# Eight gate products are issued before 32 up products instead of behind them

## The chip, the cores and the metric

The kernel runs on one core of a Trainium2 chip. The metric is the device time of one execution in microseconds (us). The engines of the core are TensorE (PE, with its weight loads as PEld), VectorE (DVE), ScalarE (ACT), GpSimd (POOL) and SyncE (SP), which issues the transfers. Each of ACT, DVE and POOL carries out its instructions in the order in which the program lists them.

## The reference

Three layers follow each other on 2 sequences of 768 tokens: a recurrent attention (mLSTM, 8 heads of 40), a gated MLP with a spatial mix (gMLP), and a channel mix. What matters here is the second layer, and that the third uses it:

```python
h = np.maximum(x @ w_in, 0.0)                       # x: (2, 768, 320), w_in: 320 x 1024
u, v = h[..., :512], h[..., 512:]
mu, var = np.mean(v, -1, keepdims=True), np.mean((v - mu) ** 2, -1, keepdims=True)
v_n = (v - mu) / np.sqrt(var + 1e-06)
v_s = np.einsum('ts,bsd->btd', w_spatial, v_n) + b_spatial[None, :, None]
x = (u * v_s) @ w_out                               # w_out: 512 x 320
# channel mix: token shift, k = relu(xk @ w_k)**2, out = sigmoid(xr @ w_r) * (k @ w_v)
```

## The kernel before

The kernel computes in float32 by pairs: each operand of a product is split into a high half (rounded to the form that TensorE takes) and a low half (what is left), and a product is a sum of high*high, high*low and low*high. So each input of a product needs two writes: a cast by ACT (high) and a subtraction by POOL or DVE (low).

The tokens come in 12 chunks of 128. Chunks 0 to 5 are sequence 0, chunks 6 to 11 are sequence 1; the attention takes them in the order 0, 6, 1, 7, ... 5, 11. When a chunk's attention output is transposed (`turn`), two kinds of product become possible:

- **vp** (`vpart`, one per chunk, 8 matmuls of 512 columns): x @ w_in's second half. Behind it runs a chain: ACT relu from PSUM into `vr` (L718), DVE statistics (L705, L720), POOL root (L710, L711), DVE normalise (L724), ACT cast to the high half of `vn` (L726), POOL subtraction for its low half (L234, out `vn`). `vr` has two buffers.
- **up** (`upart`, four per pair of chunks, 8 matmuls of 256 columns each): the first half of w_in, with one ACT relu into `u` (L739).

They lie in a list, `fillers`, one entry per matmul, and are issued one or a few at a time between the attention's steps. An entry holds the function, its planned cost (0.229 us for a vp matmul, 0.107 for an up matmul), and the keys it must wait for. When the attention has issued its last step, what is left in the list is issued at once. At that point these are: the rest of vp4, vp10, vp5, the four up products of the pair (4, 5), called up2, then vp11, then the four of the pair (10, 11), called up5.

Before they go out, the kernel queues the splitting of w_out (`widen("w_o", ...)`, four pieces; name `wo`). A piece comes as raw bits by a transfer into one of two `wraw` buffers; ACT and DVE turn it to float32 (L273, L274, L278, L282), ACT casts it to the high half (L290), POOL subtracts (L234, out `wo`). The tiles `wo` take pages of a ring of 12, and the first write to them (the cast of piece 0) waits for the last reader of the page it takes over: that is a matmul of vp11, which reads the high half of w_in's second half (`w_v`) there.

Behind the last up comes the spatial mix, four runs `s0` to `s3` of four products `spp`, 18 matmuls each: `s0` and `s1` (both halves of w_spatial) read the six `vn` chunks of sequence 0, `s2` and `s3` those of sequence 1. In a product the low half of chunk 5 is read last, by matmul 18, and its high half first by matmul 16. The whole order is `s0 K1 s1 r o0 K0 s2 v x o1 s3 o2`: `o` is the w_out product (`wop`), `K`, `r` and `v` queue the splitting of w_k, w_r and w_v. The second half of w_spatial (`wsp`, six pieces, also through `wraw`) is split during `s0`. Then come the channel mix's products `kp`, `rp` and, last, `vv` with w_v.

The order of work of the four compute engines is written out by a planner inside the kernel: it keeps a clock for each engine from estimated costs (the first number of every step), and issues the step of the chain that can start first. The order on ACT, DVE and POOL thus follows from the order in which TensorE's products are put out.

The products take eight PSUM banks in turn, six from one pool and two from another; a bank is free when the ACT or DVE step that reads it is done.

Of the kernel before, what the change touches and what calls it, by code (L numbers as in the profile page):

```python
# [17 lines left out]
def tile_mlstm_gmlp_channelmix(  # L18
# [64 lines left out]
    class Chain:  # L83
# [14 lines left out]
        def eta(self, k):  # L98
            t = self.ready
            for s in self.steps:  # L100
                t = max(t, free.get(s[0], 0.0)) + s[1] + HOP
                if len(s) > 3 and s[3] == k:
                    break
            return t
# [70 lines left out]
    def finish(*keys, stall=True):  # L175
        for k in keys:
            while any(b[0] == k or b[0][0] == k for b in back):
                if not force_feed():
                    break
            for c in [c for c in running if c.has(k)]:  # L180
                while c in running and c.has(k):
                    advance(c.start(), skip=c)
                    if not c.open():
                        finish(split[0], stall=False)
                    if c in running and c.has(k):
                        issue(c)
        if stall:
            at_least(max([done.get(k, 0.0) for k in keys], default=0.0))
# [246 lines left out]
    def arrival(i):  # L435
        return max(st["at", i], st["rows", i, 0] - 0.9) if i is not None else 0.0
# [343 lines left out]
    fillers = []  # L780

    later = []

    def fill(n, lag=1e9):
        for _ in range(n):
            if fillers and eta(fillers[0][2]) > clock[0] + lag:
                break
            if not fillers and later:
                fillers.extend(later)
                later.clear()  # L790
            if fillers:
                fillers.pop(0)[0]()
# [194 lines left out]
    while todo:  # L987
# [9 lines left out]
        if best is None:  # L997
            if fillers and eta(fillers[0][2]) <= clock[0] + 0.1:
# [3 lines left out]
                        key=lambda t: max(eta(t["keys"]), arrival(t["arrive"])))  # L1002
# [21 lines left out]
    for j in range(4):  # L1024
        widen("w_o", wo[0][:, j, :DM], ((wo[1][:, j, :2 * P], slice(0, 2 * P)), (wo[0][:, j, DM:], slice(2 * P, DM))), w_out[j])
    closing.append(0)
    fill(len(fillers) + len(later))
    finish(*[c.key for c in running if not c.late], stall=False)

    at.release()  # L1030
# [298 lines left out]
```

## Time and profile before

| what | value |
|---|---|
| median of 3 runs | 313.67 us (313.42 to 313.88) |
| profiled execution, own time | 313.5 us |
| its span, first to last instruction | 311.8 us |
| PE busy | 298.6 us, 96% of the span |
| PEld busy | 283.4 us, 91% |
| DVE / ACT / POOL busy | 71% / 53% / 49% |
| mean granted TensorE clock | 0.982 |
| chain that ended last, share of PE | 80% |

The span is what the trace covers; the execution's own time has 1.7 us more. The chain that ended last is followed back from the last instruction to whatever released each step; where it names an engine other than PE, that engine held TensorE up.

### The profile page before, as it was taken

The numbers are of one execution on the slowest core, as the hardware profiler recorded it, in microseconds if no ns is written. First come the engines' busy times: TensorE is split into PE (matmuls) and PEld (weight loads), VectorE is DVE, ScalarE is ACT, GpSimd is POOL, SyncE is SP. The second block draws the span as 40 slices with busy tenths as digits, with TensorE's granted clock in tenths as the row PEclk, the third lists the DMA queues.
The fourth block names the chain that finished last, engine by engine and source line by source line (L and its number), as shares of the span: only waits on it lengthen the run. The fifth ranks groups of instructions, "written<-read, shape, count | busy, mean of one in ns | idle before, by whom it ended". The sixth has DMA issues, their size and how long they took to land.

```text
span 311.8 us, 5519 instructions
## 1 busy us (share of the span) xinstructions
PE 298.6 (96%) x2010; PEld 283.4 (91%) x2010; DVE 220.8 (71%) x432; ACT 165.6 (53%) x348; POOL 153.5 (49%) x197
## 2 busy tenths in 40 slices
PE   8899987799999999979999999999999999999995
PEld 6777876698988998979999999999999999999994
DVE  7799895764658668466798999898867755745611
ACT  3645778534746533453444474586955744734610
POOL 5174557933768944582483736563625404403500
PEclk9999999599999999979999999999999999999999
DMA  5959663343341301135222511231010010001001
GB/s 153 300 163 312 224 230 98 114 115 110 91 144 52 125 30 39 47 126 178 104 84 62 182 44 52 79 125 42 3 41 26 0 42 23 0 23 42 0 23 43
DMA packets 13938, 28.75 MB, mean 92 GB/s; under 512 B 2407, under 2 KB 7783, under 8 KB 13911
## 3 DMA queue, kind: packets, MB, share of 16 engines
q1 hardware_dynamic: 13879, 28.33, 29.3%
q8 instruction: 16, 0.26, 0.4%
q0 software_dynamic: 32, 0.07, 0.1%
q14 instruction: 11, 0.09, 0.1%
HBM read 26.20 MB, written 1.97 MB: 90 GB/s over the span
## 4 chain that ended last, share of the span: by engine, by line
PE 80%; DVE 6%; ACT 4%; POOL 4%; issue 2%; DMA 1%; SPq 1%; DVEq 0%; ACTq 0%; POOLq 0%
PE spp L649 16%; PE kp L649 14%; PE vv L649 14%; PE wop L649 7%; PE up L649 6%; PE vp L649 5%; PE rp L649 5%; PE av L576 4%; PE sc L456 2%; PE ip L556 2%; PE sp L522 2%; PE ld L487 1%; DMA og<-in_o_tok_dram 1%; POOL vn L234 1%; PE tp L624 1%
## 5 line engine op out<-in xcount | busy, mean ns | idle before, releaser
L649 PE MATMUL spp<-wsp,vn 128*128 128x384 f32 x288 | 52.6, 342 | 1.6 <-ACT vn L726 0.8
L649 PEld LDWEIGHTS spp<-wsp,vn 128*128 128x128 f32 x288 | 51.4, 193 | 2.2 <-ACT vn L726 1.2
L1172 POOL TENSOR_TENSOR sq<-sq 128x384 f32<-128x384 f32 x32 | 29.9, 940 | 47.2 <-ACT sq L1171 47.2
L649 PE MATMUL kp<-xk,wk 128*128 128x384 f32 x256 | 45.3, 334 | 0.0
L649 PEld LDWEIGHTS kp<-xk,wk 128*128 128x128 f32 x256 | 44.4, 188 | 0.0
L649 PE MATMUL vv<-wv,k 128*128 128x320 f32 x288 | 42.9, 309 | 0.0
L649 PEld LDWEIGHTS vv<-wv,k 128*128 128x128 f32 x288 | 42.4, 188 | 0.0
L234 DVE TENSOR_TENSOR k<-sq,k 128x384 fp32r<-128x384 f32 x32 | 26.2, 820 | 13.6 <-ACT k L1173 13.6
L1069 POOL TENSOR_TENSOR vs<-vs,u 128x384 f32<-128x384 f32 x16 | 19.8, 1244 | 19.7 <-DVE vs L1068 19.7
L649 PE MATMUL up<-xg,w_u 128*128 128x256 f32 x192 | 29.2, 291 | 0.0
L649 PE MATMUL vp<-w_v,xg 128*128 128x512 f32 x96 | 28.4, 410 | 0.1
L278 DVE SCALAR_TENSOR_TENSOR wbits<-wsq,wbits 128x320 int32<-128x320 int32 (+1 forms) x27 | 22.3, 829 | 6.0 <-ACT wsq L273 5.2
L649 PEld LDWEIGHTS up<-xg,w_u 128*128 128x128 f32 x192 | 25.4, 190 | 0.5
L576 PE MATMUL av<-kvq,dt 128*128 128x123 f32 (+1 forms) x192 | 25.6, 279 | 0.1
L576 PEld LDWEIGHTS av<-kvq,dt 128*128 128x128 f32 x192 | 24.7, 197 | 1.0 <-issue 0.3
L1171 ACT ACTIVATE sq<-kp 128x384 f32<-128x384 f32 x32 | 15.6, 490 | 16.2 <-PE kp L649 14.1
L649 PE MATMUL wop<-gt,wo 128*128 128x384 f32 x128 | 22.8, 334 | 0.0
L649 PEld LDWEIGHTS wop<-gt,wo 128*128 128x128 f32 x128 | 22.2, 188 | 0.0
L649 PEld LDWEIGHTS vp<-w_v,xg 128*128 128x128 f32 x96 | 17.1, 189 | 3.0 <-DVE xg L234 0.5
L1212 DVE TENSOR_TENSOR ob<-rs,vv 128x320 f32<-128x320 f32 x12 | 5.8, 487 | 19.7 <-PE vv L649 18.7
L234 POOL TENSOR_TENSOR vn<-vr,vn 128x512 fp32r<-128x512 f32 x12 | 15.8, 1313 | 5.4 <-ACT vn L726 5.3
L282 DVE SCALAR_TENSOR_TENSOR wsq<-wraw,wbits 128x320 int32<-128x320 int32 (+1 forms) x21 | 18.2, 870 | 0.3
(182 smaller groups left out, 565.9 us busy)
## 6 DMA issues: line engine op xcount, KB each, us to landing
kvq<-in_kvq_dram SPq DMA_DIRECT2D x10, 516.0 KB
qk<-in_qk_dram SPq DMA_DIRECT2D x24, 160.0 KB
wraw<-in_w_k_dram SPq DMA_DIRECT2D x6, 512.0 KB
wraw<-in_w_v_dram SPq DMA_DIRECT2D x8, 320.0 KB
wraw<-in_w_sp_dram SPq DMA_DIRECT2D x12, 192.0 KB
og<-in_o_tok_dram SPq DMA_DIRECT2D x12, 160.0 KB
out_dram<-ob SPq DMA_DIRECT2D x12, 160.0 KB
w_inv<-in_w_in_dram SPq DMA_DIRECT2D x3, 512.0 KB
```

The source lines that it names most:

```text
L234: eng.tensor_tensor(out=out, in0=a, in1=b.bitcast(F32), op=ALU.subtract)
L278: vec.scalar_tensor_tensor(out=t["bits"], in0=t["sq"].bitcast(I32), scalar=3, in1=t["bits"], op0=ALU.logical_shift_left, op1=ALU.bitwise_or)
L282: vec.scalar_tensor_tensor(out=t["sq"].bitcast(I32), in0=t["high"], scalar=SIGN, in1=t["bits"], op0=ALU.bitwise_and, op1=ALU.bitwise_or)
L456: pe.matmul(st["sc", i, x][:, h * P:(h + 1) * P], k_[64 * x:64 * x + D, h, :], q_[64 * x:64 * x + D, h, :], start=True, stop=True)
L522: pe.matmul(sp[:n * D, h0 * DA:(h0 + n) * DA], kw[:, h0:h0 + n, :].rearrange("p h d -> p (h d)"), vt[:, h0:h0 + n, :].rearrange("p h d -> ...
L556: pe.matmul(ip[:, h0 * DA:(h0 + n) * DA], qt[:n * D, g, :], cs[:n * D, h0 * DA:(h0 + n) * DA], start=True, stop=True)
L576: pe.matmul(av[:, own_, :], A[:, h, :], vt[:, own_, :], start=True, stop=True)
L649: pe.matmul(out[0], l, x, start=j == 0, stop=j == len(prs) - 1)
L1069: ("P", 1.29, lambda: pool.tensor_tensor(out=vs, in0=vs, in1=ut[b][:, d, sl], op=ALU.mult)),
L1171: chain(("k2", g, f), ("A", 0.49, lambda: act.activation(out=sq, in_=ps, func=AF.Relu), ("kp", g, f)), ("P", 0.96, lambda: pool.tensor_ten ...
L1172: ("P", 0.96, lambda: pool.tensor_tensor(out=sq, in0=sq, in1=sq, op=ALU.mult)),
L1212: vec.tensor_tensor(out=ob, in0=rs, in1=ps, op=ALU.mult)
```

## The change

Where the rest of the list is issued, it is now sorted first: from the first entry that begins a product or waits for something, all entries with a planned cost of 0.2 or more (the vp matmuls) go ahead of those below (the up matmuls). The sort keeps the order within each kind.

```diff
     closing.append(0)
-    fill(len(fillers) + len(later))
+    rest = fillers + later
+    begun = next((x for x, f in enumerate(rest) if f[2]), 0)
+    fillers.clear()
+    later.clear()
+    fillers.extend(rest[:begun] + sorted(rest[begun:], key=lambda f: f[1] < 0.2))
+    fill(len(fillers))
     finish(*[c.key for c in running if not c.late], stall=False)
```

On TensorE, behind vp5, this is the first product before (up2_0; the number behind a name is a tile's own):

```order
L649 MATMUL vp5_1622<-w_v1_149,xg2_1338 128x512
L649 MATMUL up2_0_1652<-xg2_1338,w_u0_623 128x256
L649 MATMUL up2_0_1652<-xg2_1338,w_u1_624 128x256
L649 MATMUL up2_0_1652<-xg2_1338,w_u0_623 128x256 x2
L649 MATMUL up2_0_1652<-xg2_1338,w_u1_624 128x256
```

And at the same place after:

```order
L649 MATMUL vp5_1622<-w_v1_149,xg2_1338 128x512
L649 MATMUL vp11_1652<-w_v0_148,xg5_1457 128x512
L649 MATMUL vp11_1652<-w_v1_149,xg5_1457 128x512
L649 MATMUL vp11_1652<-w_v0_148,xg5_1457 128x512 x2
L649 MATMUL vp11_1652<-w_v1_149,xg5_1457 128x512
L649 MATMUL vp11_1652<-w_v0_148,xg5_1457 128x512 x2
L649 MATMUL vp11_1652<-w_v1_149,xg5_1457 128x512
L649 MATMUL up2_0_1678<-xg2_1338,w_u0_623 128x256
```

Only vp11 has moved: ahead of the 32 matmuls of up2. Behind up5 the products are the same as before.

On ACT, from the relu of vp5 (`vr5`) to the cast of chunk 5's high half (`vn1_0<-vr5`), before:

```order
L718 ACTIVATE vr5_1650<-vp5_1622 128x512
L739 ACTIVATE u0_942<-up2_0_1652 128x256
L739 ACTIVATE u0_942<-up2_1_1661 128x256
L726 CAST vn3_0_1497<-vr10_1618 128x512
L273 ACTIVATE wsq_1693<-wraw_1642 128x320
L739 ACTIVATE u0_942<-up2_2_1676 128x256
L290 CAST wo0_1590<-wsq_1629 128x320
L739 ACTIVATE u0_942<-up2_3_1690 128x256
L290 CAST wo0_1590<-wsq_1693 128x320
L273 ACTIVATE wsq_1727<-wraw_1668 128x320
L718 ACTIVATE vr11_1722<-vp11_1708 128x512
L726 CAST vn1_0_1348<-vr5_1650 128x512
```

And after:

```order
L718 ACTIVATE vr5_1650<-vp5_1622 128x512
L290 CAST wo0_1590<-wsq_1629 128x320
L726 CAST vn3_0_1497<-vr10_1618 128x512
L273 ACTIVATE wsq_1672<-wraw_1642 128x320
L718 ACTIVATE vr11_1676<-vp11_1652 128x512
L739 ACTIVATE u0_942<-up2_0_1678 128x256
L739 ACTIVATE u0_942<-up2_1_1687 128x256
L739 ACTIVATE u0_942<-up2_2_1699 128x256
L290 CAST wo0_1590<-wsq_1672 128x320
L739 ACTIVATE u0_942<-up2_3_1714 128x256
L726 CAST vn1_0_1348<-vr5_1650 128x512
```

The relu of vp11 (`vr11`) stood directly ahead of that cast and behind two preparations of w_out pieces (`wsq_1693`, `wsq_1727`); it now stands ahead of the four relus of up2, and the preparation of the last piece has gone behind the cast.

On POOL, from the low half of chunk 10 (`vn3_1<-vr10`) to the low half of chunk 5 (`vn1_1<-vr5`), before:

```order
L234 TENSOR_TENSOR vn3_1_1498<-vr10_1618,vn3_0_1497 128x512
L710 TENSOR_TENSOR sb5_1651<-sb5_1651,eps_71 128x1
L711 TENSOR_TENSOR sb5_1651<-sb5_1651,eps_71 128x1
L234 TENSOR_TENSOR wo1_1591<-wsq_1629,wo0_1590 128x256
L234 TENSOR_TENSOR wo0_1590<-wsq_1629,wo0_1590 128x64
L234 TENSOR_TENSOR wo1_1591<-wsq_1693,wo0_1590 128x256
L234 TENSOR_TENSOR wo0_1590<-wsq_1693,wo0_1590 128x64
L234 TENSOR_TENSOR vn1_1_1349<-vr5_1650,vn1_0_1348 128x512
```

And after:

```order
L234 TENSOR_TENSOR vn3_1_1498<-vr10_1618,vn3_0_1497 128x512
L710 TENSOR_TENSOR sb5_1651<-sb5_1651,eps_71 128x1
L711 TENSOR_TENSOR sb5_1651<-sb5_1651,eps_71 128x1
L710 TENSOR_TENSOR sb11_1677<-sb11_1677,eps_71 128x1
L711 TENSOR_TENSOR sb11_1677<-sb11_1677,eps_71 128x1
L234 TENSOR_TENSOR wo1_1591<-wsq_1629,wo0_1590 128x256
L234 TENSOR_TENSOR wo0_1590<-wsq_1629,wo0_1590 128x64
L234 TENSOR_TENSOR vn1_1_1349<-vr5_1650,vn1_0_1348 128x512
L234 TENSOR_TENSOR vn3_1_1498<-vr11_1676,vn3_0_1497 128x512
```

Between the two subtractions stood two pairs of w_out (pieces 1 and 2); now the root of chunk 11 (`sb11`) and one pair stand there, and chunk 11's low half follows at once.

## Rows read from the trace of the kernel before

**Rows 1.** The chain that ended last: start us, us, engine, tile, line, count.

```profile
121.84 3.83 PE up L649 x32
...
127.33 0.47 ACT wo L290
...
136.15 23.89 PE spp L649 x127
...
165.59 12.48 PE spp L649 x72
...
221.79 10.56 PE vv L649 x72
```

**Rows 2.** PE's instructions in time, idle time before them in brackets.

```profile
131.19 2.77 PE L649 MATMUL spp<-wsp,vn 128*128 128x384 f32 x15
134.80 0.62 PE L649 MATMUL spp<-wsp,vn 128*128 128x384 f32 x2 [0.84 <-ACT vn L726]
136.15 14.01 PE L649 MATMUL spp<-wsp,vn 128*128 128x384 f32 x70 [0.73 <-POOL vn L234]
```

**Rows 3.** Stretches: us, busy of five engines (instructions), granted clock, DMA share, GB/s.

```profile
131.19:134.00 2.81, 2.77 (x17) 2.45 (x15) 1.87 (x4) 1.19 (x3) 2.81 (x5) 1.00 0.24 70
136.15:138.00 1.85, 1.85 (x8) 1.85 (x9) 0.91 (x3) 1.02 (x3) 1.30 (x3) 0.73 0.25 52
138.00:139.00 1.00, 1.00 (x5) 1.00 (x4) 0.43 (x1) 0.54 (x2) 0.61 (x2) 0.50 0.91 321
...
140.00:141.00 1.00, 1.00 (x7) 1.00 (x6) 1.00 (x2) 0.15 (x1) 0.43 (x1) 0.79 0.09 32
141.00:142.00 1.00, 1.00 (x7) 1.00 (x6) 0.97 (x3) 0.36 (x1) 0.01 (x1) 1.00 0.18 18
```

**Rows 4.** ACT's instructions in time, round the casts of wo and vn.

```profile
127.33 0.46 ACT L290 CAST wo<-wsq 128x320 fp32r<-128x320 f32 x1 [4.77 <-PE vp L649]
127.69 0.59 ACT L718 ACTIVATE vr<-vp 128x512 f32<-128x512 f32 x1
...
133.27 0.49 ACT L273 ACTIVATE wsq<-wraw 128x320 f32<-128x320 f32 x1 [1.11 <-POOL wo L234]
...
134.14 0.61 ACT L726 CAST vn<-vr 128x512 fp32r<-128x512 f32 x1
```

**Rows 5.** POOL's instructions in time, in the same stretch.

```profile
123.15 1.30 POOL L234 TENSOR_TENSOR vn<-vr,vn 128x512 fp32r<-128x512 f32 x1
127.87 1.02 POOL L234 TENSOR_TENSOR wo<-wsq,wo 128x256 fp32r<-128x256 f32 x2 [3.42 <-ACT wo L290]
...
130.67 0.44 POOL L710 TENSOR_TENSOR sb<-sb,eps 128x1 f32<-128x1 f32 x1
131.19 0.88 POOL L711 TENSOR_TENSOR sb<-sb,eps 128x1 f32<-128x1 f32 x1
...
134.83 1.27 POOL L234 TENSOR_TENSOR vn<-vr,vn 128x512 fp32r<-128x512 f32 x1 [0.37 <-ACT vn L726]
```

**Rows 6.** DVE's instructions in time, in the same stretch.

```profile
121.37 0.53 DVE L724 TENSOR_SCALAR vr<-vr,sb 128x512 f32<-128x512 f32 x1
...
122.80 0.49 DVE L282 SCALAR_TENSOR_TENSOR wsq<-wraw,wbits 128x320 int32<-128x320 int32 x1
123.21 1.52 DVE L724 TENSOR_SCALAR vr<-vr,sb 128x512 f32<-128x512 f32 x1
...
134.89 1.56 DVE L282 SCALAR_TENSOR_TENSOR wsq<-wraw,wbits 128x320 int32<-128x320 int32 x1
```

**Rows 7.** ACT's last cast and DVE's last subtraction of w_spatial's second half.

```profile
145.07 0.51 ACT L776 CAST wsp<-wraw 128x384 fp32r<-128x384 f32 x1 [0.72 <-DMA wraw<-in_w_sp_dram]
...
145.62 0.56 DVE L234 TENSOR_TENSOR wsp<-wraw,wsp 128x384 fp32r<-128x384 f32 x1 [0.67 <-ACT wsp L776]
```

**Rows 8.** POOL's last pieces of w_v, DVE's split of xk.

```profile
227.43 1.74 POOL L234 TENSOR_TENSOR wv<-wsq,wv 128x320 fp32r<-128x320 f32 x2 [3.90 <-ACT wv L290]
...
228.82 1.75 DVE L234 TENSOR_TENSOR xk<-tm,xk 128x768 fp32r<-128x768 f32 x2 [1.23 <-ACT xk L1115]
```

## The prediction

> **What bounds the kernel now.** I read the chain that ended last first. From 136.15 us to its end TensorE is in it without a break worth naming, so up to there a microsecond counts only where TensorE stands still or runs slowly. Just ahead, the chain leaves TensorE: behind vp11 it goes to ACT's first cast of w_out at 127.33 and comes back at 136.15 with the spatial products spp [rows 1]. TensorE was in fact busy for most of that time: it issued up5, and then 15 matmuls of spp at 131.19, 2 more at 134.80 and the rest from 136.15. The two gaps end with ACT's cast of `vn` and POOL's subtraction for `vn` [rows 2]: chunk 5's high and low half, which matmuls 16 and 18 of the first spp product read.
>
> What these gaps cost is read off a run that has none. `s2`, 72 matmuls of the same shape, took 12.48 us, or 0.1733 each; so `s0` and `s1` together should take 24.96. They took from 131.19 to 136.15 + 23.89 = 160.04 [rows 1, 2], 28.85: 3.89 too much. The 15 matmuls were done at 131.19 + 15 x 0.1733 = 133.79, so the first gap is 1.01; the two were done at 135.15, so the second is 1.00. The other 1.88 us come from the clock. It was granted in full up to 134.00; after the gaps it fell, stood at 0.50 (1.2 GHz) in the stretch from 138 to 139, and was full again (2.4 GHz) from 141 [rows 3].
>
> Then the question is why chunk 5 was late. Its vp5 was done before up2 began at 121.84 [rows 1], over 12 us ahead of the gap. But ACT stood still for 4.77 us ahead of 127.33, in front of the first cast of w_out, until vp11 had read the last of the page that this cast overwrites; the relu of vp5 was next in ACT's queue, at 127.69 [rows 4]. The rest of the chain follows from there: chunk 5's cast at 134.14 and its subtraction from 134.83 to 136.10 [rows 4, 5].
>
> **The change, step by step.** TensorE has the same matmuls; only vp11 and the 32 of up2 trade places, so no work is added. up2 took 3.83 us [rows 1], and vp11 ends that much earlier: the cast of w_out can start at 127.33 - 3.83 = 123.50. What is behind it on ACT (vp5's relu, chunk 10's cast, all of up2's relus) is released with it.
>
> Is chunk 5 then in time? From the cast to the end of its subtraction the kernel before needed 136.10 - 127.33 = 8.77; shifted, that is 132.27. Two corrections. The relu of vp5 needs the `vr` buffer that POOL reads until 123.15 + 1.30 = 124.45 [rows 5]; before, it came 0.36 behind the cast, which would be 123.86, so 0.59 is added. On POOL, the root of chunk 11 (0.44 + 0.88) now stands ahead of chunk 5's subtraction, and one pair of w_out's subtractions (1.02) has gone [rows 5]: 0.30 more. That makes 133.16. I give no credit for ACT's 1.11 of waiting for POOL at 133.27 [rows 4], which stood ahead of the cast and now stands behind it. Matmul 18 starts at 131.19 + 17 x 0.1733 = 134.14, so chunk 5 is 0.98 early. The cast, before done at 134.75, comes at 131.51 by the same shift, 2.3 ahead of matmul 16 at 133.79.
>
> The bounds: a normalise step of DVE took 0.53 alone and 1.52 beside a POOL subtraction [rows 6]. If chunk 5's is stretched by that 0.99, its subtraction ends at 134.15 and TensorE waits 0.01; with no correction at all it ends 1.9 early. So both gaps go, and with them the clock's fall: -1.01 - 1.00 - 1.88 = -3.89.
>
> Moving vp11 costs TensorE nothing by itself. Its relu now waits for POOL to finish chunk 10, and the four relus of up2 stand behind it in ACT's queue. But the first spp product reuses the PSUM bank of up2's first product, so that relu has until 131.19; five instructions of at most 0.6 [rows 4] and one POOL subtraction of 1.30 [rows 5] behind 124.45, it starts before 129. SP's queue: the transfers of w_spatial's second half wait for the `wraw` buffer that DVE's last step of w_out frees at 134.89 + 1.56 = 136.45 [rows 6], so they move with DVE.
>
> **What is late next.** The engines beside TensorE do not shift by 3.89 as a matter of course. Between `s0` and the channel mix they are driven by the splitting of weights, whose start is the last piece of w_spatial: cast at 145.07, subtracted until 146.18, both behind a transfer [rows 7]. Call S the amount by which this piece comes earlier. The next product that then runs short is the first vv. It began at 221.79, with 72 matmuls in 10.56, 0.1467 each [rows 1]; its 56th, at 229.86, reads the low half of w_v's seventh piece, the first of the two that POOL wrote from 227.43, 0.87 each: 228.30 [rows 8]. The slack is 1.56. TensorE gets there 3.89 earlier, so it waits 3.89 - 1.56 - S = 2.33 - S. (xk for the next product is complete at 230.57 [rows 8], 1.78 ahead of that product at 232.35 [rows 1]: looser.)
>
> S is not in the trace. The most is the full shift, 3.83. The least is worked out from DVE's last step of w_out: in the new order it stands beside the subtractions of chunks 5 and 11; if it can end only behind both, that is 133.16 + 1.30 + 0.49 = 134.95 against 136.45, so S = 1.5. I take 2.2, nearer the lower end, since this very instruction is seen stretched, 1.56 where its like took 0.49 at 122.80 [rows 6]. That leaves a wait of 0.13. With S at 1.5 it is 0.83, with S above 2.33 nothing.
>
> At 123.21 the normalise step ended 0.28 behind the POOL subtraction that had begun 0.06 ahead of it [rows 5, 6]. The Trainium skill (SBUF — State Buffer, section Who interferes with whom) speaks against this change here: a VectorE instruction with two SBUF inputs, or in a mode that uses both ports, is held for the whole of a GpSimd instruction that reads SBUF, if that one began first. By that rule, with which the row agrees, S is at its lower end of 1.5 and the sum is 310.4; by the short durations of DVE alone S is the full 3.83 and the sum 309.6.
>
> The sum, against the profiled execution's own 313.5 (span 311.8): 313.5 - 3.89 + 0.13 = **309.7**. The median of the runs shown is 313.67, so the same change from there would be 309.9.
>
> **The rivals.**
> - *The clock falls all the same.* It fell only some 2 us behind the second gap's start, and no row shows what made it fall; if it was not the gaps, only 2.01 are won: 311.5. Against it: no other stretch behind 136 shows it, and none has a gap.
> - *The win is partly given back in vv.* S is below 2, because DVE's and POOL's steps collide more than I allow or because the transfers are no earlier: a wait of 0.4 to 2.3, 310.0 to 311.9. For it: DVE's stretched steps [rows 6].
> - *The change doesn't do what it says*: the root of chunk 11 and its statistics, now ahead of chunk 5's on DVE and POOL, hold chunk 5 up, spp pauses again by up to 1 us and the clock falls: 309.6 + 1.0 + 1.88 = 312.5 or more. Against it: 0.98 of slack.
> - *Slower.* The weights are no earlier at all (S = 0) and the pause in vv, then 2.33, halves the clock as the two gaps in `s0` did: 2.33 + 1.88 = 4.21 against 3.89, which is 313.8. It decides from S below 0.3, for then the time is above 313.5. Against it: the buffer that starts these transfers is free at least 1.5 earlier.
>
> **How the numbers follow.** The forecast 0.70, with its own range 309.2 to 310.4; given back in vv 0.12; the clock 0.08; chunk 5 still late 0.05; slower 0.05. The predicted time is 309.7. The range 309.1 to 311.6 leaves out the last two and the far end of the second. 0.2% of the time, 0.63 us, is about what a measurement of this kernel can tell from no change: faster means below 312.9, slower above 314.1. The first three cases and half of the fourth are faster, 0.92; of the slower case I put 0.04 beyond 314.1 and the rest, with the other half of the fourth, near no change, 0.04.
>
> **What would show it.** Right: ACT's first cast of w_out starts near 123.5; vp5's relu near 124.5; the first spp product has no gap and the granted clock is 1.00 from 131 to 160; `s0` and `s1` take about 25.0 us; the first wop starts near 156.2; w_spatial's last subtraction ends 1.5 to 3.8 earlier than 146.18. Wrong: a gap in front of matmul 16 or 18 of the first spp; a stretch at 0.50 in a run without gaps; a wait of TensorE in the first vv for POOL's `wv`, larger than 0.8.

## The result, and the profile after

The changed kernel takes 310.96 us (median of 8 runs, 310.06 to 312.18) against 313.55 for the kernel before on the same chip (8 runs, 312.49 to 314.63): a ratio of 0.9916, 95% interval 0.9893 to 0.9939. Two later sets of runs gave 310.91 against 313.03 and 310.42 against 313.01. (The products that the title counts are matmuls: the eight of vp11 and the 32 of up2.) The profiled execution took 311.12 for a span of 309.4.

The chain that ended last, in the changed kernel (start us, us, engine, tile, line, count), against [rows 1]:

```profile
118.17 6.38 PE vp L649 x28
124.55 7.67 PE up L649 x64
132.22 24.96 PE spp L649 x144
...
226.25 0.91 POOL wv L234
...
227.20 2.77 PE vv L649 x17
229.97 11.12 PE kp L649 x64
```

The first two spp products are one piece of 24.96 us, exactly twice the 12.48 of `s2`; the detour over ACT's cast of w_out is gone. But the chain now leaves TensorE at another place, in the first vv, for POOL's split of w_v.

PE's instructions in time at the same place, against [rows 2]:

```profile
132.06 25.13 PE L649 MATMUL spp<-wsp,vn 128*128 128x384 f32 x144
```

Stretches of it, with the granted clock in the column behind the five engines, against [rows 3]:

```profile
134.00:136.00 2.00, 2.00 (x13) 2.00 (x12) 1.40 (x1) 0.74 (x3) 2.00 (x3) 1.00 0.00 0
136.00:138.00 2.00, 2.00 (x14) 2.00 (x13) 0.78 (x1) 0.69 (x3) 1.60 (x4) 1.00 0.73 221
138.00:139.00 1.00, 1.00 (x7) 1.00 (x6) 0.53 (x1) 0.44 (x1) 0.00 (x0) 1.00 0.99 366
```

No gap, and 1.00 where 0.50 stood. Measured alike in both traces, `s0` and `s1` went from 28.85 to 25.13: 3.72 us won there, 2.01 of gaps and 1.71 of clock.

The clock's part holds for these two executions, not for each. Of the kernel before, the later sets give the mean granted clock of 46 executions. The fall of [rows 3] takes about 0.0055 off it (0.50 from about 137.0 to 140.4, in a span of 311.8). 27 have 0.981 to 0.983, like the profiled one; 8 have 0.986; 11 have 0.989, as high as in traces where that fall is missing, and these are on average 0.4 to 1.1 us faster than the 27 of the same set. Of 20 executions of the changed kernel, 18 have 0.987 to 0.989 and two 0.983 and 0.984 (311.62 and 312.30 us; no trace shows where). So the fall is frequent in the kernel before and rare in the changed one.

ACT, round the casts, against [rows 4]:

```profile
124.36 0.46 ACT L290 CAST wo<-wsq 128x320 fp32r<-128x320 f32 x1 [0.91 <-PE vp L649]
125.37 0.60 ACT L718 ACTIVATE vr<-vp 128x512 f32<-128x512 f32 x1 [0.55 <-POOL vn L234]
...
130.64 0.61 ACT L726 CAST vn<-vr 128x512 fp32r<-128x512 f32 x1
```

The wait of 4.77 in front of the first cast of w_out is 0.91, and the relu of vp5 follows 1.01 behind it. DVE's last steps on w_out and its last piece of w_spatial, against [rows 6, 7]:

```profile
132.89 1.04 DVE L278 SCALAR_TENSOR_TENSOR wbits<-wsq,wbits 128x320 int32<-128x320 int32 x1 [0.74 <-ACT wsq L273]
134.03 1.40 DVE L282 SCALAR_TENSOR_TENSOR wsq<-wraw,wbits 128x320 int32<-128x320 int32 x1
...
144.43 0.56 DVE L234 TENSOR_TENSOR wsp<-wraw,wsp 128x384 fp32r<-128x384 f32 x1 [1.96 <-ACT wsp L776]
```

POOL, from chunk 11's root on, and at w_v's last pieces, against [rows 5, 8]:

```profile
130.13 0.40 POOL L710 TENSOR_TENSOR sb<-sb,eps 128x1 f32<-128x1 f32 x1 [0.90 <-DVE sb L720]
130.61 0.55 POOL L711 TENSOR_TENSOR sb<-sb,eps 128x1 f32<-128x1 f32 x1
131.13 1.21 POOL L234 TENSOR_TENSOR wo<-wsq,wo 128x256 fp32r<-128x256 f32 x2
132.29 2.79 POOL L234 TENSOR_TENSOR vn<-vr,vn 128x512 fp32r<-128x512 f32 x2
...
226.25 1.73 POOL L234 TENSOR_TENSOR wv<-wsq,wv 128x320 fp32r<-128x320 f32 x2 [3.90 <-ACT wv L290]
```

Here is what was given back. The two chunk subtractions stand on POOL from 132.29 to 135.08, and DVE's last two steps on w_out stand beside them; the last ends at 135.43, only 1.02 earlier than the 136.45 of before. That step frees the buffer for w_spatial's transfers; the last piece of w_spatial is subtracted at 144.99 (146.18 before), and the last pieces of w_v start at 226.25 (227.43 before). TensorE came 3.72 us earlier, less the 0.87 by which this execution lagged already at vp4 (116.74 against 115.85); the weights came 1.2 earlier.

The span's 2.4 us are therefore: 3.72 won in `s0` and `s1`, 0.47 lost in the first vv, and 0.87 of a later start. The last is variation between executions: programs whose work on TensorE is the same up to there reached vp4 at 115.34 to 116.74 in the eleven profiles of this study, the changed kernel itself at 116.74, 116.00 and 115.50.

### The profile page after: what moved, and what is told of

It is laid out like the page before. It is cut to its first block, busy times and chain, and to the rows that moved or that the text cites. A ratio compares the mean times of both kernels' runs of the same rounds, so it can differ in the third digit from the quotient of the medians.

```text
span 309.4 us, 5521 instructions
## 1 busy us (share of the span) xinstructions
PE 298.2 (96%) x2010; PEld 283.1 (91%) x2010; DVE 220.6 (71%) x432; ACT 166.1 (54%) x348; POOL 152.8 (49%) x197
## 4 chain that ended last, share of the span: by engine, by line
PE 76%; DVE 6%; ACT 5%; POOL 5%; issue 3%; DMA 2%; SPq 1%; DVEq 0%; POOLq 0%; ACTq 0%
PE spp L649 16%; PE kp L649 11%; PE vv L649 11%; PE up L649 8%; PE vp L649 5%; PE av L576 5%; PE wop L649 5%; PE rp L649 3%; PE sc L456 3%; POOL sq L1177 2%; PE ip L556 2%; DMA qk<-in_qk_dram 2%; PE sp L522 2%; PE ld L487 1%; PE tp L624 1%
## 5 line engine op out<-in xcount | busy, mean ns | idle before, releaser
L649 PE MATMUL spp<-wsp,vn 128*128 128x384 f32 x288 | 50.4, 334 | 0.0
L649 PEld LDWEIGHTS spp<-wsp,vn 128*128 128x128 f32 x288 | 49.9, 188 | 0.0
```

Source lines behind the costliest of these rows:

```text
L649: pe.matmul(out[0], l, x, start=j == 0, stop=j == len(prs) - 1)
```

## The experiments

The theory: chunk 5 was late only because ACT, which works in order, stood in front of a cast of w_out that had to wait for vp11; the clock fell because of the two gaps that followed; and what the first vv waits for is set by when w_spatial's last piece is done. The rivals: the order of the products matters in itself; the clock's fall has another cause; the wait in vv, or the later start, is chance.

**The cast taken away, the products left as before.** The splitting of w_out is queued behind w_spatial's second half; TensorE's order is that of the kernel before.

```diff
-    for j in range(4):
-        widen("w_o", wo[0][:, j, :DM], ...
...
+    def wo_all():
+        for j in range(4):
+            widen("w_o", wo[0][:, j, :DM], ...
...
-    for a in 'h s0 K1 s1 r o0 K0 s2 v x o1 s3 o2'.split():
-        dict(h=lambda: wsp_half(1, r1), r=wr_all, v=wv_all, ...
+    for a in 'h w s0 K1 s1 r o0 K0 s2 v x o1 s3 o2'.split():
+        dict(h=lambda: wsp_half(1, r1), w=wo_all, r=wr_all, v=wv_all, ...
```

> TensorE's product order is that of the kernel before (up2 ahead of vp11); only the splitting of w_out is queued behind the second half of w_spatial, so that no cast of w_out stands in ACT's queue in front of chunk 5. Theory (ACT, in order, waited with chunk 5 behind a cast of w_out that needed vp11; the gaps, and the clock's fall behind them, came from that alone): ACT has no wait of about 4.8 us any more, the relu of vp5 starts within 1 us of vp5's end, the first spp product has no gap, the granted clock stays at 1.00, and s0 and s1 together take 24.9 to 25.3 us where before took 28.85. The time is 2.5 to 3.7 us below before on the same chip (309.9 to 311.1 from 313.55), the rest depending on how long the first vv waits for POOL's wv, 0 to 1.2 us. Rival 1 (the order of the products itself matters, for the clock or for chunk 5): the gaps of about 1.0 each or the stretch at half clock stay, s0 and s1 take 26.8 us or more, and the time is within 1 us of before. Rival 2 (w_out is now too late for wop): the first wop starts more than 0.3 us behind s1's end.

Measured: 315.24 against 313.03, ratio 1.0073 (1.0050 to 1.0096): slower. PE's instructions in time:

```profile
131.41 25.13 PE L649 MATMUL spp<-wsp,vn 128*128 128x384 f32 x144
...
226.90 0.41 PE L649 MATMUL vv<-wv,k 128*128 128x320 f32 x1 [2.01 <-ACT wv L290]
228.39 3.02 PE L649 MATMUL vv<-wv,k 128*128 128x320 f32 x18 [1.08 <-POOL wv L234]
232.08 1.44 PE L649 MATMUL vv<-wv,k 128*128 128x320 f32 x8 [0.68 <-POOL wv L234]
```

With vp11 where it had been, the gaps are gone, the clock stayed at 1.00, and `s0` with `s1` takes the same 25.13 as in the changed kernel: rival 1 falls, and chunk 5 was late because of w_out's splitting. This edit takes away the wait of the cast and w_out's pieces on ACT, DVE and POOL together; the changed kernel keeps most of those pieces ahead of chunk 5 and shortens the wait alone, so the two runs together point to the wait. The first wop did not wait either (rival 2). The time expected was wrong all the same: ACT, DVE and POOL now do w_out's work behind 140, together with all that vv needs. From 131 to 138 POOL is busy for 3.08 of 7 us, where it was for 5.96 before; from 146 to 160 for 10.04 of 14, where it was for 7.13. The last piece of w_v is split from 231.01, and TensorE stands in vv for three waits. Behind them the granted clock stayed at 1.00 in this execution, although the first two, 2.01 and 1.08 with one matmul between, are longer than the gaps of before; in 7 of its 10 executions the mean clock is lower, 0.968 to 0.984 against 0.988.

**The same with the changed order of products.** The edit above, made in the changed kernel instead of the one before.

> The changed kernel's order of products and w_out split behind the second half of w_spatial. Theory: chunk 5 has more slack still, no gap, clock 1.00, s0 and s1 25.1 us as in the changed kernel; the second half of w_spatial is split several us earlier (its last subtraction ended at 144.99 there), and if the wait of 0.46 us in the first vv comes from how late the weights' splitting starts, it goes only if w_out's pieces, now behind, do not push the later ones back: time 310.3 to 311.0 against 310.96 of the changed kernel. Rival (the sum of the work of ACT, DVE and POOL between s0 and vv sets the wait, not its order): the wait in vv stays within 0.3 us of 0.46 and the time is that of the changed kernel.

Measured: 314.33, ratio 1.0053 (1.0028 to 1.0079); the same three waits in vv, w_v's last piece again from 231.02. Neither time that was expected came, nor the wait near 0.46 of the rival. So it is where w_out's split stands that costs here, whatever TensorE's order. In this profile too the clock stayed at 1.00 behind the waits in vv.

**vp11 in the middle of up2.**

```diff
-    fillers.extend(rest[:begun] + sorted(rest[begun:], key=lambda f: f[1] < 0.2))
+    late = [f for f in rest if f[3] == 5 and f[1] > 0.2][-8:]
+    rest = [f for f in rest if not any(f is x for x in late)]
+    ups = [x for x, f in enumerate(rest) if f[1] < 0.2]
+    fillers.extend(rest[:ups[16]] + late + rest[ups[16]:])
```

> vp11 goes out in the middle of up2, behind its 16th matmul: 1.92 us later than in the changed kernel, 1.92 earlier than before. Theory: the first cast of w_out and all of chunk 5's chain come 1.9 us later than in the changed kernel; its subtraction, which ended there at about 133.7 with matmul 18 of the first spp due at 135.0, ends at about 135.6, so one gap of 0.6 us or less is left, where before had two of 1.0. If the clock falls only behind gaps as long as those of before, s0 and s1 take 25.1 to 25.8 us; if any gap there makes it fall, about 27.6. The weights come up to 1.9 later than in the changed kernel, so the first vv waits 0.4 to 1.7 us for POOL's wv. Time 0.1 to 1.9 us above the changed kernel, 311.1 to 312.8. Rival (the order of the products matters and not the wait of the cast): vp11 behind any matmul of up2 keeps both gaps and the clock's fall, 313 or more.

Measured: 310.97, ratio 0.9922 (0.9899 to 0.9946): the time of the changed kernel. PE's instructions in time:

```profile
131.46 3.12 PE L649 MATMUL spp<-wsp,vn 128*128 128x384 f32 x17
135.16 22.29 PE L649 MATMUL spp<-wsp,vn 128*128 128x384 f32 x127 [0.58 <-POOL vn L234]
...
219.03 10.72 PE L649 MATMUL vv<-wv,k 128*128 128x320 f32 x72
```

And DVE's in the same run:

```profile
132.05 0.49 DVE L278 SCALAR_TENSOR_TENSOR wbits<-wsq,wbits 128x320 int32<-128x320 int32 x1 [0.28 <-ACT wsq L273]
132.65 0.85 DVE L282 SCALAR_TENSOR_TENSOR wsq<-wraw,wbits 128x320 int32<-128x320 int32 x1
...
142.16 0.56 DVE L234 TENSOR_TENSOR wsp<-wraw,wsp 128x384 fp32r<-128x384 f32 x1 [0.55 <-ACT wsp L776]
```

The one gap came as expected (131.46 + 17 x 0.1733 = 134.41 to 135.16: 0.75, of which the trace puts 0.58 down to waiting), and the clock stood at 1.00 behind it. But the weights were not later than in the changed kernel: w_spatial was done 2.3 us earlier (142.72 against 144.99; 1.7 earlier counted from the first spp), and vv had no wait. Here POOL took w_out's third piece ahead of the two chunk subtractions, so DVE's last two steps on w_out ran clear of them, in 0.49 and 0.85 instead of 1.04 and 1.40. What the gap cost, the missing wait in vv gave back.

**The changed kernel again, and a third time.** No edit.

> The changed kernel once more. In its first profile TensorE reached the unchanged point vp4 at 116.74 us, 0.87 later than in the profile of before (115.85), though both programs are the same up to there. Theory (that is jitter of the start): the mean of its runs against before on the same chip is 2.6 to 3.7 us faster, and the profile reaches vp4 anywhere from 115.7 to 117. Rival (the change itself costs those 0.9 us, by code or memory laid out differently): vp4 is reached at 116.5 or later again, and the difference stays at 2.6 or less.

> The changed kernel beside the two below on one chip. Theory (the side engines pin the first vv, TensorE's own start does not matter for it): the next kp product starts at 229.9 to 230.1, as in both earlier profiles (229.97, 230.07), wherever TensorE reached vp4 (116.74 and 116.00 there), and the last two pieces of w_v start at 226.2 to 226.4. Time 310.9. Rival (the wait is jitter of TensorE's start alone): kp moves with vp4.

Measured: 310.91 and 310.42, as given above. The chain at the first vv, the second time:

```profile
226.36 0.90 POOL wv L234
...
227.31 2.76 PE vv L649 x17
230.07 11.10 PE kp L649 x64
```

And the third time:

```profile
225.56 0.90 POOL wv L234
...
226.51 2.76 PE vv L649 x17
229.26 11.10 PE kp L649 x64
```

The first of these sets is 2.1 us below before (means 310.94 and 313.04), not the 2.6 to 3.7 expected. TensorE reached vp4 at 116.00 and 115.50, so the late start was not the change's. Two of the six executions are those with a mean clock of 0.983 and 0.984; the other four are 2.6 below.

The wait in vv is there each time. The third profile does not bear out that kp has a fixed place (229.9 to 230.1 expected, 229.26 came); what stays the same is the distance from w_spatial's last subtraction to w_v's last pieces, as the table below shows.

**Chunk 11 last.** TensorE's order is that of the changed kernel; chunk 11, which only the third spp product reads, is given to the planner 4 us later.

```diff
-                  ("A", 0.52, lambda: act.copy(hi, vr)), ("P", 1.23, lambda: sub(pool, lo, vr, hi)))
+                  ("A", 0.52, lambda: act.copy(hi, vr)), ("P", 1.23, lambda: sub(pool, lo, vr, hi)),
+                  ready=clock[0] + 4.0 if i == 11 else None)
```

> The changed kernel, with chunk 11's chain of relu, statistics, root, normalise, cast and subtraction given to the planner 4 us later; chunk 11 is read only by the third spp product. TensorE's list is that of the changed kernel. POOL now subtracts w_out's second and third piece ahead of chunk 5, and chunk 11 last of all, so DVE's two steps on w_out's last piece no longer stand beside two chunk subtractions. Theory (DVE's steps held by POOL's chunk subtractions made w_out's last step late, 135.43, that held w_spatial's transfers, and the first vv's wait for wv follows 81.3 us behind w_spatial's last subtraction): those two steps take under 0.9 us each where they took 1.04 and 1.40, the last of them ends by 133.5, w_spatial's last subtraction ends by 143.5 instead of 144.99, the last two pieces of w_v start by 225 instead of 226.25, and the first vv has no wait. No gap in the first spp either. Time 0.4 to 1.3 us below the changed kernel: 309.6 to 310.5. Rival (the sum of the engines' work sets the wait in vv): the last two pieces of w_v still start within 0.3 us of 226.25, and the time is that of the changed kernel.

> Chunk 11's chain 4 us later in the plan, once more, beside the changed kernel on one chip: the first time it had 310.47 against 310.91 to 310.96, with no wait in vv and one of 0.33 in up5. Theory: 0.3 to 1.0 us below the changed kernel, that is the wait in vv (0.46 and 1.31 in its two profiles) less 0.33. Rival (no difference that can be measured): within 0.2 of the changed kernel.

Measured: 310.47, ratio 0.9908 (0.9889 to 0.9927), and 310.64, 0.9926 (0.9900 to 0.9952), where the changed kernel had 310.42 on the same chip: no gain that the times can show, and in the second set not the 0.3 to 1.0 expected. PE's instructions in the first of the two profiles:

```profile
130.18 1.21 PE L649 MATMUL up<-xg,w_u 128*128 128x256 f32 x8 [0.33 <-ACT u L740]
```

DVE's last step on w_out in it:

```profile
131.25 1.58 DVE L282 SCALAR_TENSOR_TENSOR wsq<-wraw,wbits 128x320 int32<-128x320 int32 x1
```

And POOL, at chunk 5 and at w_v's last pieces:

```profile
131.19 1.29 POOL L234 TENSOR_TENSOR vn<-vr,vn 128x512 fp32r<-128x512 f32 x1 [0.63 <-ACT vn L726]
...
223.77 1.74 POOL L234 TENSOR_TENSOR wv<-wsq,wv 128x320 fp32r<-128x320 f32 x2 [3.90 <-ACT wv L290]
```

The chain of causes holds: w_spatial is done at 142.48, w_v's pieces start at 223.77, and the wait in vv is gone. One link was missed: DVE's last step is not short, it ran beside chunk 5's subtraction and took 1.58, only earlier. And a new wait of 0.33 stands in up5, whose PSUM bank ACT empties later.

**Chunk 11 2 us later.** Against the run before:

```diff
-                  ready=clock[0] + 4.0 if i == 11 else None)
+                  ready=clock[0] + 2.0 if i == 11 else None)
```

> Chunk 11's chain 2 us later in the plan instead of 4: POOL subtracts w_out's third piece ahead of chunks 5 and 11, which then follow each other, and the fourth behind them, as in the run with vp11 in the middle of up2, but with vp11 ahead of up2. Theory: w_spatial's last subtraction ends at 142 to 144, the last pieces of w_v start by 225, no wait in the first vv, no gap in spp, and the relus of up2 stand closer behind vp11's, so that the wait of 0.33 in up5 goes or stays below 0.33: 310.0 to 310.6, at least 0.3 below the changed kernel. Rival (two chunk subtractions in a row hold DVE's steps on w_out's last piece as in the changed kernel): w_out's last step ends past 135, and vv waits as there.

Measured: 309.78, ratio 0.9903 (0.9876 to 0.9930), the lowest median of all; 0.64 below the changed kernel on the same chip, with intervals that overlap. DVE's instructions in time:

```profile
130.80 0.86 DVE L282 SCALAR_TENSOR_TENSOR wsq<-wraw,wbits 128x320 int32<-128x320 int32 x1
...
140.29 0.56 DVE L234 TENSOR_TENSOR wsp<-wraw,wsp 128x384 fp32r<-128x384 f32 x1 [0.47 <-ACT wsp L777]
```

POOL's, and the first vv on PE:

```profile
131.81 2.72 POOL L234 TENSOR_TENSOR vn<-vr,vn 128x512 fp32r<-128x512 f32 x2
...
222.94 1.71 POOL L234 TENSOR_TENSOR wv<-wsq,wv 128x320 fp32r<-128x320 f32 x2 [3.90 <-ACT wv L290]
```

```profile
217.79 10.72 PE L649 MATMUL vv<-wv,k 128*128 128x320 f32 x72
```

The last step on w_out ends at 131.66, ahead of both chunk subtractions, and TensorE has no wait from vp11 to the end of the trace that is worth naming. This version beats the kernel before clear of noise. Against the changed kernel the profile shows a reason for being faster, and the times make it probable, not certain.

**vp11 behind three quarters of up2, and one up product issued twice.** Against the run with vp11 in the middle:

```diff
-    fillers.extend(rest[:ups[16]] + late + rest[ups[16]:])
+    fillers.extend(rest[:ups[24]] + late + rest[ups[16]:])
```

The second index was left at 16. So up2's third product (entries 17 to 24) is in the list twice, ahead of vp11 and again behind it, and the run does not do what was set out:

> vp11 goes out behind the 24th of up2's 32 matmuls: 0.96 us later than in the run with it in the middle, 0.96 earlier than before. What is asked is how long a gap has to be here for the clock to fall: one gap of 0.75 in front of matmul 18 left it at 1.00, two of 1.01 and 1.00 with 2 matmuls between them did not. Theory: the first cast of w_out starts 0.9 to 1.0 later than there (about 126.6); the gaps in the first spp are 0.3 to 1.8 us together, and s0 and s1 take 25.1 plus these; if the clock falls, another 1.5 to 2 us. Time 311.3 to 313.2. Rival (the fall in before had nothing to do with the gaps, but with what ACT, POOL or the transfers did at 137 to 140): the clock stays at 1.00 with gaps as long as those of before, or falls with none.

Measured: 314.64, ratio 1.0040 (1.0022 to 1.0058). The up matmuls on the profile's page, before and in this run:

```profile
L649 PE MATMUL up<-xg,w_u 128*128 128x256 f32 x192 | 29.2, 291 | 0.0
```

```profile
L649 PE MATMUL up<-xg,w_u 128*128 128x256 f32 x200 | 31.8, 301 | 2.5 <-ACT u L739 2.5
```

PE's instructions in time, and the relu on ACT that they wait for:

```profile
128.78 7.50 PE L649 MATMUL up<-xg,w_u 128*128 128x256 f32 x48 [2.53 <-ACT u L739]
136.12 25.13 PE L649 MATMUL spp<-wsp,vn 128*128 128x384 f32 x144
```

```profile
126.06 0.46 ACT L290 CAST wo<-wsq 128x320 fp32r<-128x320 f32 x1 [3.81 <-PE vp L649]
...
128.34 0.39 ACT L739 ACTIVATE u<-up 128x256 f32<-128x256 f32 x1
```

The clock by stretches, from the gap on:

```profile
126.30:128.78 2.48, 0.00 (x0) 0.00 (x0) 1.30 (x4) 2.48 (x8) 1.64 (x3) 1.00 0.00 0
128.78:130.00 1.22, 1.22 (x8) 1.22 (x9) 1.11 (x2) 0.30 (x1) 1.14 (x3) 0.80 0.00 0
130.00:131.00 1.00, 1.00 (x7) 1.00 (x6) 0.79 (x3) 0.60 (x2) 1.00 (x2) 0.50 0.00 0
...
132.00:133.00 1.00, 1.00 (x6) 1.00 (x6) 0.84 (x3) 1.00 (x3) 1.00 (x2) 0.54 0.22 81
133.00:134.00 1.00, 1.00 (x11) 1.00 (x10) 0.59 (x3) 1.00 (x4) 0.85 (x2) 1.00 0.08 16
```

The gap is not where it was expected, and it is made by the repeated product. In the kernel's source an up product keeps its PSUM bank, so the second time it writes where its first result lies, and waits, for 2.53, until ACT's relu has read that at 128.73; the relu stands behind the late cast of w_out. The eight extra matmuls cost another 0.96 (8 x 0.1198). The time of this run therefore says nothing of vp11 at that place.

It still shows a fall of the clock at another time than before, with other transfers and other neighbours. The 48 matmuls went from 128.78 to the first spp at 136.12, 7.34, where 64 take 7.67 at full clock, so 5.75 for 48: 1.59 lost, near the 1.71 of before. But the rival on the clock does not fall with it. In 3 of its 10 executions the mean clock is 0.989, in the other 7 it is 0.984, and these are 1.25 slower on average. And the granted clock in 40 equal slices, in tenths of full speed, in the profiles of before, of this run and of the run with w_out's splitting behind w_spatial:

```profile
PEclk9999999599999999979999999999999999999999
```

```profile
PEclk9999999599999999799999999999999999999999
```

```profile
PEclk9999999599999999999999999999999999999999
```

The third has the three waits in vv, near slice 29, and no fall behind them. The 5 near 55 to 62 us stands, as 5 or 6, in all eleven profiles; TensorE waits for 2.8 there. So TensorE stood still ahead of each fall that was seen, but standing as long did not always bring one. What else decides stays open.

Side by side: the start of the first spp in time, end of w_spatial's last subtraction, S (how much earlier that end comes than before, counted from the first spp; before it lies 14.99 behind), start of w_v's last two pieces, and how long the first vv is held up (the start of the next kp in the chain less that of the first spp, less 97.44, as in the runs without a wait or a gap). The two runs that split w_out later are left out, as w_out's work stands between there.

| kernel | first spp | w_spatial done | S | w_v pieces | from done to w_v | vv held up |
|---|---|---|---|---|---|---|
| before | 131.19 | 146.18 | 0 | 227.43 | 81.25 | 0 |
| after | 132.06 | 144.99 | 2.06 | 226.25 | 81.26 | 0.47 |
| after again | 131.32 | 145.08 | 1.23 | 226.36 | 81.28 | 1.31 |
| after, third | 130.82 | 144.32 | 1.49 | 225.56 | 81.24 | 1.00 |
| vp11 in the middle | 131.46 | 142.72 | 3.73 | 224.18 | 81.46 | 0 |
| chunk 11 last | 131.23 | 142.48 | 3.74 | 223.77 | 81.29 | 0 |
| chunk 11 last, again | 131.36 | 142.60 | 3.75 | 223.86 | 81.26 | 0 |
| chunk 11 2 us later | 131.08 | 140.85 | 5.22 | 222.94 | 82.09 | 0 |
| vp11 at three quarters, one product twice | 136.12 | 144.20 | 6.91 | 227.97 | 83.77 | 0 |

(The gap of the middle run and the loss of 28.85 against 25.13 before are no waits of vv and are left out of the last column.) From w_spatial's last subtraction to w_v it is 81.2 to 81.3 us in six of nine rows, and hold-up plus S is 2.53, 2.54 and 2.49 in the three that wait. Where S is largest the distance grows; in the last two rows w_v's pieces start 91.86 and 91.85 behind the first spp, so there TensorE's own products seem to set them.

## Why the prediction was right, and where not

*Chunk 5 in time, both gaps and the clock's fall gone* (-3.89): right. That the gaps hang on the cast's wait is shown by the cast's start against that of the first spp: 7.70 ahead no gap (the changed kernel), 5.79 ahead one of 0.75 (vp11 in the middle), 3.86 ahead 2.01 (before). The size is 3.72: the start of `s0` was taken from the list in time, which lies 0.16 ahead of the chain's, but the 12.48 of `s2` from the chain, so the clock's share is 1.71 and not 1.88. That share belongs to the profiled execution; 11 of 46 have no such fall by their mean clock. Nor was the clock granted in full all the way up to 134.00: it stood at 0.50 from about 55 to 62, in both kernels alike. Chunk 5 was forecast 0.98 early; its cast came at 130.64 and POOL's subtractions from 132.29, the first of two in 2.79, with matmul 18 due at 135.01, so it was some 1.3 early.

*The first vv waits 2.33 - S*: right in form. Measured it is 2.53 - S. The 0.16 between list and chain stands in the 3.89 and in the slack of 1.56 alike and cancels. The rest is 0.08 less slack (POOL took 0.91 for the piece and TensorE started 0.04 behind it) and 0.12 for the matmuls behind the wait, which was not counted: in the changed kernel the 17 matmuls from 227.20 took 2.61 up to the next kp, at 229.81 in the list in time, where 17 x 0.1467 is 2.49.

*S taken as 2.2*: this is the step that failed. Measured: 2.06, 1.23, 1.49, mean 1.59, so near the lower end of 1.5 and once well below it, and the hold-up is 0.9 on average instead of 0.13. In two of the three profiles it is above the 0.8 that was set down as a sign of being wrong. The lower end had been worked out from just what then happened: DVE's last step on w_out ends behind both chunk subtractions, 135.43 behind 135.08. No reason was given for stopping above it; the one that was given, that the very instruction is seen stretched, speaks for the lower end itself. The rule of the Trainium skill (SBUF — State Buffer, section Who interferes with whom), by which a DVE instruction with two SBUF inputs is held for the whole of a POOL instruction that began first, agrees with the traces here: the step ended 0.35 behind POOL's subtraction in the changed kernel, and 0.35 behind it again with chunk 11 last (132.83 behind 132.48). By it the sum had been 310.4.

The sum with the measured terms is 313.5 - 3.72 + 0.94 = 310.7, against medians of 310.42 to 310.96. So it was the second rival, the win partly given back in vv, that came; the range held the time, the likeliest case's own range of 309.2 to 310.4 did not quite. A fall of the clock without a gap, chunk 5 still late and the slower case are in none of the three profiles; two of the 20 executions have a mean clock that fits a fall, and no trace of them was taken. No one foresaw a start that varies by over 1 us between executions; it blurs single spans.

*Moving vp11 costs TensorE nothing*: right for this change, with no wait in up5. It is no general truth: with chunk 11's relu 4 us later, up waits for its PSUM bank by 0.33.

## What to carry to other kernels

A gap in one engine may be made by an in-order queue far from it: look at what stands in front of the late instruction in its own engine's queue, and for whom that waits. When such a gap goes, work out what is late next from the engines beside, and take stretched steps seen in the trace at their stretched length. Moving work out of the idle time of the engines beside costs later what it saves at first.

## What was not expected of the hardware

What stood ahead of a fall of TensorE's clock, by the profiles: behind one gap of 0.75 it stayed at 1.00; behind two of 1.01 and 1.00 with two matmuls between, it was 0.50 (1.2 GHz) from about 137.0 to 140.4; behind one of 2.53 it was 0.50 from about 129.5 to 132.9; behind 2.01 and 1.08 with one matmul between, in the first vv of the run that splits w_out later, it stayed at 1.00. And one program has the fall in some executions and not in others: by the mean clock, 3 of 10 and 11 of 46 are without it. A trace of one execution does not tell how often. The two falls cost 1.71 and 1.59 on top of the gaps (3.72 - 2.01, and 7.34 - 5.75).

A row's idle time can be less than what a wait costs. In the changed kernel the wait in vv reads 0.19, but the 56th matmul was due at 218.78 + 55 x 0.1467 = 226.85 and started at 227.20, 0.35 late: the rows in time reach some 0.16 past the start of the next (132.06 + 25.13 = 157.19, where the next product's row starts at 157.03). With the 0.12 of the matmuls behind it that is 0.47.
